# Where ten symmetry tests run: four of them moved from one block's down projection to those of two earlier blocks

## The chip, the cores and the metric

One core of one Trainium2 chip runs the whole program. Its engines work side by side, each through its own list of instructions in order, and wait for each other by semaphores: PE (matrix products into PSUM), DVE and ACT (element-wise work on SBUF and PSUM), POOL (here mostly the issuing of DMAs), SP (DMAs alone). The metric is the device time of one execution in microseconds (us); before the change the median of 3 runs is 1126.09 us (1125.63 to 1129.37).

## The reference

Two equal layers act on x, 2048 tokens of 640 numbers in float32. Each layer is a Fourier mixing and a gated feed-forward network, both behind a layer norm and with a residual:

```
def _A_ref(x, dft_seq_re, dft_seq_im, dft_hid_re, dft_hid_im):
    a = jnp.einsum("bsd,ed->bse", x, dft_hid_re)
    b = jnp.einsum("bsd,ed->bse", x, dft_hid_im)
    return jnp.einsum("ts,bse->bte", dft_seq_re, a) - jnp.einsum("ts,bse->bte", dft_seq_im, b)

def _B_ref(x, w_gate, w_up, w_down):
    g = jnp.einsum("bsd,df->bsf", x, w_gate)
    u = jnp.einsum("bsd,df->bsf", x, w_up)
    h = _sigmoid(g) * u
    return jnp.einsum("bsf,fd->bsd", h, w_down)

x = x + _A_ref(_layernorm(x), ...)      # twice, with the same matrices
x = x + _B_ref(_layernorm(x), ...)
```

The two sequence matrices are 2048 x 2048 and come as inputs; F is 1728. The kernel uses that a Fourier matrix repeats itself with changed signs along rows and columns and multiplies by folded, smaller matrices. It tests on the chip that the given matrices have these symmetries: it loads the parts that should be equal up to sign, subtracts or adds them, and sums the squares of what is left. All tests together set one flag at the end; if it says that the symmetry does not hold, a plain, unfolded version runs behind it (with the inputs given it does not). No matrix product waits for a single test.

## The kernel before, in words

**Staging.** A layer has a Fourier part and then a feed-forward part in four blocks of 512 tokens. I count layers and blocks from 1 in the text; the code counts from 0, so that layer 1's blocks are (0, 0) to (0, 3). A block goes through 14 gate and up steps (the products on line 1531; step 0 to 13 of the block) and then through its "down": 8 steps that multiply by the third weight (L1743), two to a row tile of 128 tokens. In layer 1's block 4 two sequence steps stand in between. A down step takes PE 5.6 us; the downs of layer 1 run at about 176 to 220, 300 to 345, 425 to 470 and 553 to 598 us.

**What follows a down.** L1758 on DVE adds each finished row tile from PSUM to X, in two halves. Then the block is folded for layer 2's Fourier part: statistics (L534 and L535, or L768 and L770 for a half), their root on POOL (L516) with small steps around it (L515 to L529), sums and differences of columns (L787, L788), coefficients (L793 and before it L828, L829), scaled rows on ACT (L840, L842) and DVE (L845, L849), and the join (L929 on DVE, L939 on ACT, L949 on DVE), whose result PE multiplies on L1088. In the next block's gate steps L1572, L1580, L1600 on DVE and L1589 on ACT take products out of PSUM and make the gated product of them; L1572 is the one that empties banks for PE.

**The order.** A function at(u, f) puts the job f on a clock of steps: u is a position in PE's order, and each engine gets its instructions in the order of these positions. Nothing else sets the order, neither a cost nor a due time.

**The tests.** The table TESTS gives 84 tests a place: layer, block, step of the load, step of the test, step of the square. The tests stand in a fixed list (32 of rows, 10 of columns, then 32 and 10 again for the second matrix), and the table's entries are given to them in this order. A row test loads 4 x 128 KB by DMAs that POOL issues (L1916), DVE works on them (L1922, L1923, L1925 twice) and ACT squares and sums (L1888). A column test loads 2 x 256 KB (L1933) and has L1939 to L1942 on DVE. Both need a "room" of SBUF for their data from load to square. Two rooms are fixed; if neither is free when a load is placed, one more is taken from the big tile, out of the space where the other tiles live. A later load into a room waits for the test and the square that used it before. All loads stand in order on POOL, all tests in order on DVE.

The table is used here:

```
for (load, test, key), (l, b, u, v, w) in zip(tests, TESTS):
    if l == layer:
        at(block[b] + u, load, *key)
        at(block[b] + v, test, *key)
        at(block[b] + w, square_rest)
```

Where tiles lie in the big tile is found by a planner from the times at which they are taken and dropped. A load by SP into such a place waits for the last user of the place.

Of the kernel before, what the change touches and what calls it, by code (L numbers as in the profile page):

```python
# [80 lines left out]
NP = 6  # L81
MADE = {(1, 1), (1, 2), (1, 3)}
TESTS = [(0, 1, 3.5, 4.9, 5.7), (0, 1, 4.5, 5.9, 6.7), (0, 1, 5.5, 7.1, 7.9), (0, 1, 7.38, 8.97, 9.78), (0, 1, 9.25, 10.85, 11.65), (0, 1, 11.12, 12.72, 13.53),
# [2403 lines left out]
```

## Time and profile before

| | |
|---|---|
| median of 3 runs | 1126.09 us |
| the profiled execution | 1127.29 us |
| its span | 1125.50 us |
| its mean granted clock of TensorE | 0.997 |
| busy: PE, DVE, ACT, POOL | 98%, 73%, 47%, 31% |
| DMA moved | 226.54 MB, 201 GB/s |
| row test loads (L1916), POOL | 256 issues, 128 KB each |
| column test loads, POOL | 32 issues, 256 KB each |

A row of a timeline has the start, the time from the first start to the last end, the engine, the line, the operation, the tiles out<-in with their shapes, the count, and in brackets for how long the engine had been idle before it and what ended that. A row of windows has for each stretch the busy time of each engine, then the granted clock, the mean busy share of the 16 DMA engines and the GB/s moved. A row of waits has the engine, the tile and line that waited, what it waited for, and the us in total, the number of times and the longest. The span of 1125.5 us is what the profile covers; the profiled time is 1.79 us more.

### The profile page before, as it was taken

The page shows a single profiled execution, that of the slowest core. Times are in us where ns is not written, and L with a number is a line of the kernel's source. Part 1 is how long each engine was busy: PE and PEld are TensorE (multiplying, and loading weights), DVE is VectorE, ACT ScalarE, POOL GpSimd, SP SyncE. Part 2 cuts the span into 40 slices and gives each one's busy share as a digit, 9 for nine tenths or more (in the row PEclk, how much of TensorE's full clock was granted, in tenths as well). Part 3 has the DMA queues.
Part 4 walks back from the last instruction along what each step waited for, and adds up shares of the span by engine and source line. Part 5 has one row for each costly group of instructions (what it writes and reads, how often), then busy time and mean ns, then how long its engine had stood idle before and what let it go on. Part 6 is the DMA issues. An engine that isn't in the chain of part 4 may idle for free. (4 is left out here: it accounts for less than half of the span.)

```text
span 1125.5 us, 23738 instructions
## 1 busy us (share of the span) xinstructions
PE 1104.8 (98%) x9004; PEld 881.6 (78%) x9004; DVE 827.2 (73%) x1841; ACT 532.0 (47%) x1153; POOL 345.7 (31%) x568
## 2 busy tenths in 40 slices
PE   7999999999999999999999999999999999999997
PEld 5767446788878887788877878778887888788875
DVE  7984987868877898686568877864887398827962
ACT  6975584245534654255434734422652255415530
POOL 1001654342555445243480202433530214011001
PEclk9999999999999999999999999999999999999999
DMA  7533886889598969977761674598857873398401
GB/s 237 196 103 105 303 295 208 256 260 297 204 220 245 284 208 223 266 258 240 188 200 34 183 201 160 141 254 293 258 153 157 297 244 80 99 259 232 156 7 45
DMA packets 158050, 226.54 MB, mean 201 GB/s; under 512 B 75055, under 2 KB 100161, under 8 KB 157926
## 3 DMA queue, kind: packets, MB, share of 16 engines
q1 hardware_dynamic: 139222, 176.84, 52.3%
q0 software_dynamic: 18560, 47.93, 14.8%
q8 instruction: 72, 1.18, 0.4%
q14 instruction: 52, 0.43, 0.1%
q10 hardware_dynamic: 144, 0.16, 0.0%
HBM read 180.90 MB, written 29.37 MB: 187 GB/s over the span
## 5 line engine op out<-in xcount | busy, mean ns | idle before, releaser
L1531 PE MATMUL acc<-big 128*128 128x256 f16 x4698 | 516.8, 273 | 0.8 <-DMA big<-kept_w 0.4
L1531 PEld LDWEIGHTS <-big 128*128 128x128 f16 x4698 | 459.6, 98 | 55.6 <-issue 0.8
L1916 POOL DMA_DIRECT2D big<-in_ct x256 | 174.3, 687 | 209.5 <-DVE big L1925 121.4
L1743 PE MATMUL acc<-big 128*128 128x320 f16 x1640 | 223.6, 299 | 0.0
L1535 ACT ACTIVATE big<-acc 128x256 f32<-128x256 f32 x268 | 100.7, 381 | 231.4 <-PE acc L1531 220.8
L1743 PEld LDWEIGHTS <-big 128*128 128x128 f16 x1640 | 160.5, 98 | 62.2
L1888 ACT ACTIVATE big<-big 128x768 f32<-128x768 f32 (+9 forms) x110 | 81.3, 739 | 77.6 <-DVE big L1925 61.8
L1484 PE MATMUL acc<-big 128*128 128x256 f16 (+1 forms) x705 | 114.7, 325 | 0.3 <-ACT big L730 0.3
L1788 PE MATMUL acc<-big 128*128 128x320 f16 x756 | 105.6, 299 | 0.0
L1484 PEld LDWEIGHTS <-big 128*128 128x128 f16 x705 | 68.9, 98 | 44.9 <-issue 0.6
L1788 PEld LDWEIGHTS <-big 128*128 128x128 f16 x756 | 74.0, 98 | 28.6
L323 DVE SCALAR_TENSOR_TENSOR big<-big 128x640 f16<-128x640 f32 (+8 forms) x88 | 72.1, 848 | 15.7 <-ACT big L321 10.0
L1589 ACT ACTIVATE big<-big 128x512 f32<-128x512 f32 x87 | 52.8, 628 | 63.1 <-DVE big L1580 62.8
L321 ACT ACTIVATE big<-big 128x640 f16<-128x640 f32 (+8 forms) x88 | 58.6, 698 | 24.6 <-POOL big L1390 10.9
L1600 DVE SCALAR_TENSOR_TENSOR big<-acc,big 128x256 f32<-128x256 f32 x87 | 36.3, 418 | 43.2 <-PE acc L1531 38.6
L1617 DVE TENSOR_TENSOR big<-big 128x512 f16<-128x512 f32 x51 | 35.2, 689 | 42.0 <-ACT big L1616 41.1
L1580 DVE TENSOR_TENSOR big<-big,acc 128x512 f32<-128x512 f32 x87 | 56.2, 679 | 3.2 <-PE acc L1531 2.9
L1808 DVE SCALAR_TENSOR_TENSOR big<-acc,big 128x320 f32<-128x320 f32 x48 | 23.0, 487 | 44.7 <-PE acc L1799 33.1
L494 POOL DMA_INDIRECT out<-big,rows x8 | 8.8, 1105 | 140.5 <-DMA out<-big 53.5
L1641 DVE TENSOR_TENSOR big<-big 128x512 f16<-128x512 f32 x72 | 41.2, 617 | 9.9 <-ACT big L1640 9.9
L673 ACT ACTIVATE big<-big 128x384 f16<-128x384 f32 (+2 forms) x48 | 28.6, 647 | 41.3 <-DVE big L655 29.2
L1572 DVE TENSOR_TENSOR big<-acc,big 128x256 f32<-128x256 f32 x80 | 30.4, 415 | 23.8 <-PE acc L1531 20.8
(268 smaller groups left out, 1312.4 us busy)
## 6 DMA issues: line engine op xcount, KB each, us to landing
big<-kept_s SPq DMA_DIRECT2D x84, 512.0 KB
big<-kept_w SPq DMA_DIRECT2D x115, 320.0 KB
big<-in_ct POOLq DMA_DIRECT2D x256, 128.0 KB, 5.2
big<-kept_w SPq DMA_DIRECT2D x74, 192.0 KB
kept_w<-big SPq DMA_DIRECT2D x27, 320.0 KB
big<-in_ct POOLq DMA_DIRECT2D x32, 256.0 KB, 5.7
big<-in_wd SPq DMA_DIRECT2D x25, 320.0 KB
kept_s<-big SPq DMA_DIRECT2D x13, 512.0 KB
```

The source lines that it names most:

```text
L321: nc.scalar.activation(dh, src, AF.Copy, scale=s)
L323: nc.vector.scalar_tensor_tensor(dl, src, s, dh, op0=OP.mult, op1=OP.subtract)
L1484: nc.tensor.matmul(ps, w[wp][:, d * P : (d + 1) * P], xt[:, xp, :], start=(d == 0 and wp == HI and xp == HI), stop=(d == ND - 1 and wp == LO))
L1531: nc.tensor.matmul(ps, wt, xt, start=start and n == 0, stop=n == len(todo) - 1, skip_group_check=not start)
L1535: nc.scalar.activation(dst, ps, AF.Copy)
L1580: nc.vector.tensor_tensor(v[1], v[1], both, op=OP.add)
L1589: nc.scalar.activation(v, v, AF.Sigmoid, scale=SG)
L1641: nc.vector.tensor_tensor(l, src, h, op=OP.subtract)
L1743: nc.tensor.matmul(held["pd", e][0][:, :EH], held["ht", j].parts[hp][:, i * P : (i + 1) * P], held["w", 2, j].parts[wp][:, e * EH : (e + 1 ...
L1788: nc.tensor.matmul(accs[p, n][0][:, :EH], left(m, q, hp, p), right(m, w, wp), start=start and k == 0, stop=stop and k == len(out) - 1, ski ...
L1888: nc.scalar.activation(v, v, AF.Square, accum_out=new_sum()[:p])
L1916: nc.gpsimd.dma_start(v[:, g], bass.AP(ct.tensor, (r * S + row) * S, [[P, NS], [d * S, 16], [1, P]]))
```

## The change

Four of the ten tests in the down of layer 1's block 4 go: the entries of (0, 2) in the downs become 11 instead of 9, and so do those of (0, 1). Block 4's down keeps six. In the downs of blocks 2 and 3 the distance from one test to the next is 0.82 of a step instead of 1.0; from load to test it is still 1.4 steps, to square 2.2. In block 4's down the loads were half a step apart, with the test 0.7 and the square 1.2 of a step behind; now they are 0.8 apart, the test comes 1.0 and the square 1.5 behind. By these numbers a third room is no longer needed there: the third load, 1.6 steps behind the first, comes after the first one's square.

```
         (0, 1, 13.0, 14.4, 15.2),
-        (0, 1, 14.0, 15.4, 16.2), (0, 1, 15.0, 16.4, 17.2), ... (0, 1, 21.0, 22.4, 23.2),
+        (0, 1, 13.82, 15.22, 16.02), (0, 1, 14.64, 16.04, 16.84), ... (0, 1, 21.18, 22.58, 23.38),
         ...                         (the same lines for (0, 2))
-        (0, 3, 15.6, 16.3, 16.8), (0, 3, 16.1, 16.8, 17.3), (0, 3, 16.6, 17.3, 17.8), (0, 3, 17.1, 17.8, 18.3), ... (0, 3, 20.1, 20.8, 21.3),
+        (0, 3, 15.6, 16.6, 17.1), (0, 3, 16.4, 17.4, 17.9), (0, 3, 17.2, 18.2, 18.7), (0, 3, 18.0, 19.0, 19.5), (0, 3, 18.8, 19.8, 20.3), (0, 3, 19.6, 20.6, 21.1),
```

Since the list of tests is fixed, all tests from the second down on take an earlier place: the third down gets five column tests, where before one stood in it, and the gate steps of block 4 get row tests where column tests stood. PE's order is the same. Many places in the big tile change.

POOL around block 4's down: the loads of tests (L1916), of the hidden matrices' tests (L1976), and L516 of block 4's fold at the end.

```order
-L1916 DMA big<-in_ct 128x2x128 x12
+L1916 DMA big<-in_ct 128x2x128 x28
 L1976 DMA big<-in_wh 100x4x128 x8
-L1916 DMA big<-in_ct 128x2x128 x12
-L1118 MEMSET big 128x2
-L1916 DMA big<-in_ct 128x2x128 x4
-L1118 MEMSET big 128x2 x2
-L1916 DMA big<-in_ct 128x2x128 x24
+L1916 DMA big<-in_ct 128x2x128 x8
+L1118 MEMSET big 128x2 x3
+L1916 DMA big<-in_ct 128x2x128 x16
 L516 TENSOR_TENSOR quad_77<-quad_77,half 128x2 x2
```

Behind the eight loads of L1976 stand 24 loads of row tests (six tests) instead of 40; the first row has more of them, since the columns went earlier.

DVE in block 4's down, behind L1758 of tile 0 and its statistics:

```order
 L534 BN_STATS quad_77<-big 128x6 x2
 L535 BN_AGGR quad_77<-quad_77 128x2
-L1922 TENSOR_TENSOR big<-big 128x256
-L1923 TENSOR_TENSOR big<-big 128x256
-L1925 TENSOR_TENSOR big<-big 128x128 x2
 L1922 TENSOR_TENSOR big<-big 128x256
 L1923 TENSOR_TENSOR big<-big 128x256
```

One of the four tests between tile 0 and tile 1 is gone. Two more are gone ahead of tile 0, and one of two behind L845.

DVE at the end of block 2's down: L1758 of the last tile, and the fold of the block (L534, L787, L793).

```order
 L1758 SCALAR_TENSOR_TENSOR big<-acc_65,big 128x320
 L1758 SCALAR_TENSOR_TENSOR big<-acc_483,big 128x320
-L1922 TENSOR_TENSOR big<-big 128x256
-L1923 TENSOR_TENSOR big<-big 128x256
-L1925 TENSOR_TENSOR big<-big 128x128 x2
 L534 BN_STATS quad_75<-big 128x6 x2
```

Two tests more stand ahead of the L1758 shown here, and the test that stood behind it has gone to a place behind L788.

18 rows, old and new, of the table TESTS are left out of this document.

## The prediction

> **What bounds the kernel now.** I read the page's busy shares first, then the waits of PE, then PE's timeline around its longest wait, then the timelines of the engines that this wait names.
>
> ```profile
> PE 1104.8 (98%) x9004; PEld 881.6 (78%) x9004; DVE 827.2 (73%) x1841; ACT 532.0 (47%) x1153; POOL 345.7 (31%) x568
> ...
> PE acc L1088 <- ACT big L939: 1.4, 1, 1.4
> PE acc L1088 <- DVE big L949: 0.5, 1, 0.5
> ```
>
> PE is busy in 1104.8 of 1125.5 us, so a change that leaves PE's instructions alone can win only PE's idle time and the time for which its clock is low. The diff moves symmetry tests on POOL, DVE and ACT; PE's order is the same. Of the waits inside the program the longest, 1.4 us, lies right behind layer 1's last down, where tests are taken out:
>
> ```profile
> 595.75 2.47 PE L1743 MATMUL acc<-big 128*128 128x320 f16 x17
> 598.06 1.76 PE L1173 MATMUL acc<-big 128*128 128x322 f16 x17
> 599.65 6.07 PE L1088 MATMUL acc<-big 128*128 128x256 f16 x54
> 607.13 0.39 PE L1088 MATMUL acc<-big 128*128 128x256 f16 x2 [1.42 <-ACT big L939]
> 608.02 3.05 PE L1088 MATMUL acc<-big 128*128 128x256 f16 x16 [0.50 <-DVE big L949]
> ...
> 606.00:609.20 3.20, 1.45 (x10) 0.84 (x11) 2.97 (x9) 1.50 (x4) 0.00 (x0) 1.00 0.02 5
> 609.20:612.70 3.50, 3.50 (x20) 2.53 (x18) 3.30 (x8) 2.56 (x6) 0.00 (x0) 0.51 0.00 0
> ```
>
> PE ends the down (L1743) at 598.2, has other work to 605.72, and stands 1.42 + 0.50 us until 608.02; one more small pause of 0.1 us makes 2.0. In the last two rows (time, PE busy, and near the end the granted clock) the clock is 1.00 while PE pauses and 0.51 in the 3.5 us behind it: 3.5 x 0.49 = 1.7 us more. What PE waits for is the fold of block 4, whose last links are these, on DVE and ACT:
>
> ```profile
> 577.84 0.88 DVE L1758 SCALAR_TENSOR_TENSOR big<-acc,big 128x320 f32<-128x320 f32 x2
> 582.95 0.42 DVE L1923 TENSOR_TENSOR big<-big 128x256 f32<-128x256 f32 x1 [1.66 <-DMA big<-in_ct]
> 584.91 0.43 DVE L1923 TENSOR_TENSOR big<-big 128x256 f32<-128x256 f32 x1 [0.67 <-DMA big<-in_ct]
> 587.48 0.43 DVE L1923 TENSOR_TENSOR big<-big 128x256 f32<-128x256 f32 x1 [0.90 <-DMA big<-in_ct]
> 588.36 0.88 DVE L1758 SCALAR_TENSOR_TENSOR big<-acc,big 128x320 f32<-128x320 f32 x2
> 594.38 0.89 DVE L845 SCALAR_TENSOR_TENSOR big<-big,quad 128x641 f32<-128x641 f32 x1 [1.18 <-ACT big L842]
> 595.18 0.42 DVE L1922 TENSOR_TENSOR big<-big 128x256 f32<-128x256 f32 x1
> 596.38 0.42 DVE L1922 TENSOR_TENSOR big<-big 128x256 f32<-128x256 f32 x1
> 597.58 0.88 DVE L1758 SCALAR_TENSOR_TENSOR big<-acc,big 128x320 f32<-128x320 f32 x2
> 601.11 0.47 DVE L1758 SCALAR_TENSOR_TENSOR big<-acc,big 128x320 f32<-128x320 f32 x1
> ...
> 604.80 0.65 ACT L840 ACTIVATE big<-big,coef,quad 128x321 f32<-128x321 f32 x1 [6.11 <-DVE big L793]
> 606.60 0.47 ACT L939 ACTIVATE big<-big 128x321 f16<-128x321 f32 x1
> ```
>
> L1758 adds a finished row tile of the down to X. The last one starts at 601.11, although PE was done at 598.2: DVE runs late, because the tests between its additions (L1922 to L1925) cost it time, and three of them wait 1.66, 0.67 and 0.90 us for their loads. From 601.11 the chain has almost no wait: 601.11 to 606.60 for L939, 607.07 its end, and PE goes on at 607.13.
>
> **The last down: four tests less.** A test takes DVE 596.38 - 595.18 = 1.20 us. DVE's order shows where the four are missing: two ahead of L1758 at 577.84, one of the four between 577.84 and 588.36, one of the two between L845 and 597.58. So L1758 of tile 0 comes at 577.84 - 2.4 = 575.4. Tile 1 follows 10.52 us later in the row, less 1.2 for the test; of the rest up to 3.2 us (1.66 + 0.67 + 0.90) is waiting, which a longer way from load to test can remove. That is 581.5 to 584.7. What the trace does not show is the new rhythm: square comes 1.5 steps after load, loads 0.8 apart, so the two fixed rooms are reused and no third is taken; a load now waits for the square of the test two before it. The price is set by how long a load takes:
>
> ```profile
> 574.87 16.16 POOL L1916 DMA_DIRECT2D big<-in_ct  x24
> ...
> big<-in_ct POOLq DMA_DIRECT2D x26, 128.0 KB, 2.6
> ...
> big<-in_ct POOLq DMA_DIRECT2D x256, 128.0 KB, 5.2
> ```
>
> In 574 to 592 us POOL issues 24 loads without a break, 0.67 each, and they land after 2.6 us (second row, of that window); over the whole program it is 5.2 (third row, the page's). A room's round is four issues, 2.7, the landing, the test, 1.2, and the square on ACT:
>
> ```profile
> 596.55 0.84 ACT L1888 ACTIVATE big<-big 128x768 f32<-128x768 f32 x1 [1.38 <-issue]
> 597.30 0.19 ACT L1888 ACTIVATION_READ_ACCUMULATOR big<-big 128x1 f32 x1
> ```
>
> With the square's 1.0 and a landing of 2.6 that is 7.5 us, two rooms give a test every 3.75, and three tests put tile 1 at 575.4 + 11.2 = 586.6; with 5.2 it is 10.1, 5.05 each, and 590.6. I take 584.7 to 586.6, since the 2.6 is of this very window, which will hold fewer loads. From L1758 to L845 the row needs 594.38 - 588.36 = 6.0, L845 0.8, the one test 1.2, and from tile 2's addition to the last one 601.11 - 597.58 = 3.5: at 586.6 + 11.5 = 598.1 DVE is ready for the last addition just when PE ends. So it starts at 598.3, 2.8 us before 601.11. L939 ends at 604.3, before PE gets there at 605.72. Both gaps go (2.0), and with them the slow clock (1.7), 3.7 in all for PE. DVE and ACT come only some 3.0 us earlier, and they take over a little later:
>
> ```profile
> 615.20 0.89 DVE L1241 SCALAR_TENSOR_TENSOR big<-acc,big 128x322 f32<-128x322 f32 x2
> ...
> 637.40 0.44 PE L722 MATMUL acc<-ident,big 128*128 128x128 f16 x5 [0.17 <-ACT big L730]
> ```
>
> PE's transposes at 637.40 already wait 0.17 us for a chain that starts with L1241; DVE's own queue reaches L1241 no more than 2.8 to 3.1 us earlier. So **-3.0** against this execution, with bounds 0 (tile 1 at 590.6: the last addition at 602.1) and -3.7.
>
> [...]
>
> **The second and third downs: two more tests each.** In the second down DVE's order has 15 tests ahead of the last L1758 instead of 13, and one moves behind the statistics. These loads come when the DMA is full:
>
> ```profile
> 300.30:345.00 44.70, 44.70 (x332) 32.23 (x330) 29.82 (x70) 14.60 (x28) 23.73 (x35) 1.00 0.95 247
> 424.80:469.50 44.70, 44.70 (x332) 32.23 (x330) 30.68 (x71) 14.82 (x28) 21.24 (x31) 1.00 1.06 232
> ...
> 337.33 0.43 DVE L1923 TENSOR_TENSOR big<-big 128x256 f32<-128x256 f32 x1 [1.62 <-DMA big<-in_ct]
> 342.26 0.43 DVE L1923 TENSOR_TENSOR big<-big 128x256 f32<-128x256 f32 x1 [1.52 <-DMA big<-in_ct]
> 342.72 0.49 DVE L1925 TENSOR_TENSOR big<-big 128x128 f32<-128x128 f32 x2
> 344.90 0.89 DVE L1758 SCALAR_TENSOR_TENSOR big<-acc,big 128x320 f32<-128x320 f32 x2 [1.69 <-PE acc L1743]
> 345.71 0.42 DVE L1922 TENSOR_TENSOR big<-big 128x256 f32<-128x256 f32 x1
> 353.07 0.71 DVE L1572 TENSOR_TENSOR big<-acc,big 128x256 f32<-128x256 f32 x2
> ...
> 344.84 27.35 PE L1531 MATMUL acc<-big 128*128 128x256 f16 x249
> ...
> 469.38 0.89 DVE L1758 SCALAR_TENSOR_TENSOR big<-acc,big 128x320 f32<-128x320 f32 x2 [1.79 <-PE acc L1743]
> ```
>
> DVE itself has room: 2 x 1.2 us beside 44.7 - 29.8 = 14.9 idle. The bytes have none: the DMA share of the second down is 0.95 at 247 GB/s. Two tests are 2 x 4 x 128 KB = 1.05 MB, 4.2 us. I take all of it as delay of the last L1758, since every load is in order on POOL: 349.1 instead of 344.9. Behind that addition DVE still has the statistics and then L1572, which empties two banks of the next block's first gate step; it moves from 353.78 (its end) to 358.0. PE needs these banks after 120 matmuls of L1531, at 344.84 + 120 x 27.35 / 249 = 358.0. So the slack, 4.2 us, is used up just about: **+0.3**, between 0 (bytes fit into gaps) and 4.0 (below). In the third down five tests of columns come where row tests were; DVE waits 1.79 us for PE at 469.38 and the work moved behind is the same L534 to L1572, so 4.2 + 1.8 stand against a like delay: I take 0, with the second down's upper bound.
>
> The tests' addresses move too, so kept blocks loaded by SP wait for other tests than before; such loads stand 4 us or more ahead of their use in what I looked at, and I cost them at nothing; if that cover is gone, the load's lateness falls on PE one to one.
>
> **The sum.** This execution took 1127.29 us, span 1125.50 and 1.79 around it: 1127.29 - 3.0 + 0.3 = 1124.6. The median, 1126.09, lies 1.2 below the profiled one and the fastest 1.66, about what the slow clock costs, so I take the unprofiled runs for ones without it; for them only the 2.0 us of gaps are there to win: 1126.09 - 2.0 + 0.3 = 1124.4. I say **1124.5**.
>
> **Rivals.** *All of it:* the gaps and the clock are won against the median too: 1126.09 - 3.7 = 1122.4. For it: the slow clock stands in the one trace there is. Against it: the fastest run's 1125.63.
>
> *No gain:* two rooms make the tests bound by latency, 5.2 us per load instead of 2.6; tile 1 comes at 590.6, the last L1758 at 602.1, and the wait at L939 stays: 1126 to 1127. For it: three waits for in_ct in the rows of that stage. Against it: that window's 2.6.
>
> *The slow clock has another cause* than the pause, and stays when the gaps go: 1127.29 - 2.0 + 0.3 = 1125.6 in a profiled run. For it: PE was busy for 1.45 of the 3.2 us ahead of the slow stretch, so it was never long idle. Against it: the stretch starts right behind the pauses, and the stage before it has 1.00. [...]
>
> *Slower:* DVE, which is in order, waits in the second down for test loads while the last L1758 stands behind them. The two tests at 337.33 and 342.26 are 4.93 us apart. If the two added ones keep that pace, the last ends at 343.2 + 9.9 = 353.1, L1758 is 8.2 late, and L1572 passes PE's 358.0 by 4.0; a pause longer than the one at 607 brings the slow clock again, 1.7. That is 1124.3 + 5.7 = 1130.0. It decides from a delay of 4.2 us at L1758. For it: the share of 0.95. Against it: the test at 345.71 found its data without a wait.
>
> **How the numbers follow.** Forecast 0.52, all of it 0.10, no gain 0.18, clock stays 0.08, slower 0.12. What a measurement of this kernel can tell from no change is 0.3%, 3.4 us: below 1122.7 is faster, above 1129.5 slower. The forecast, no gain and the clock's case lie within: same 0.78. Faster 0.11 is "all of it" with a little over; slower 0.11 the most of the last. The likeliest case alone reaches from 1123.2 to 1126.0; the range, with no gain and most of the stall's sizes, from 1122.0 to 1128.2.
>
> **What would show it.** Right: no wait of PE at L1088 for L939 or L949, the clock at 1.00 in 606 to 613, the last L1758 of the last down within 0.5 us of PE's end, L1758 of the second down around 349 with a PE pause at L1531 under 1 us. Wrong: PE's wait at L1088 as before (then the two rooms), a pause of PE over 2 us at the start of block 3 (then the full DMA), or a wait for kept blocks somewhere else.

## The result, and the profile after

The changed kernel takes 1143.12 us (median of 4 runs, 1139.85 to 1144.47) against 1126.91 us for the kernel before (4 runs, 1125.63 to 1129.37): a ratio of 1.0137, with an interval of 1.0108 to 1.0165. It is 16 us slower, and the forecast was 1124.5, with a range up to 1128.2. The profiled span is 1141.4 us, 15.9 more than before.

The waits of PE after the change (the line that waits, what it waits for, us in total, times, longest) show where the time is:

```profile
PE acc L1531 <- ACT big L1535: 12.4, 6, 5.2
PE acc L1088 <- DMA big<-kept_o: 1.5, 1, 1.5
PE acc L1531 <- DVE big L1572: 1.2, 2, 1.0
```

Before, L1531 waited 0.4 us for L1572 and never for L1535, and there was no wait for kept_o. L1531 are the gate and up products; ACT's L1535 empties their PSUM. The two waits at L1088 for L939 and L949, which the change was to remove, are gone. The next views are windows of the second down, of block 3's gate and up steps, of the third down and of block 4's steps, first of the kernel after:

```profile
300.00:344.70 44.70, 44.70 (x332) 32.23 (x330) 29.10 (x68) 15.53 (x30) 24.45 (x36) 1.00 0.92 227
344.70:433.60 88.90, 82.09 (x733) 72.32 (x732) 70.58 (x170) 45.46 (x100) 42.12 (x74) 0.98 0.80 241
433.60:478.30 44.70, 44.70 (x332) 32.23 (x330) 25.37 (x58) 13.55 (x25) 17.38 (x25) 1.00 0.82 168
478.30:566.90 88.60, 82.58 (x734) 72.66 (x733) 65.96 (x161) 45.92 (x105) 36.52 (x57) 0.96 0.83 258
```

and of the kernel before, the two stretches of gate and up steps (its two downs stand in the prediction):

```profile
345.00:424.80 79.80, 79.80 (x733) 71.49 (x732) 67.43 (x161) 45.40 (x98) 36.33 (x67) 1.00 0.78 241
469.50:549.40 79.90, 79.90 (x734) 71.62 (x733) 58.78 (x140) 43.95 (x97) 27.15 (x43) 1.00 0.74 241
```

The downs themselves take PE 44.70 us as before, without a pause. Block 3's steps take 88.90 instead of 79.80 (+9.1), block 4's 88.60 instead of 79.90 (+8.7), by pauses and by a lower granted clock (0.98 and 0.96 for 1.00). One thing is odd: the downs that were given more tests moved *less*. In the second it is 227 x 44.7 = 10.1 MB for 11.0 before (247), in the third 7.5 MB for 10.4 (168 and 232 GB/s). The loads came late; the mean DMA share was no higher than before (0.92 for 0.95, and 0.82 for 1.06).

PE's timeline of the kernel after, at the starts of blocks 3 and 4 and behind the last down:

```profile
348.92 9.98 PE L1531 MATMUL acc<-big 128*128 128x256 f16 x90 [0.95 <-ACT big L1535]
359.92 4.75 PE L1531 MATMUL acc<-big 128*128 128x256 f16 x42 [1.01 <-DVE big L1572]
365.23 11.95 PE L1531 MATMUL acc<-big 128*128 128x256 f16 x108 [0.57 <-ACT big L1535]
381.46 22.79 PE L1531 MATMUL acc<-big 128*128 128x256 f16 x192 [4.29 <-ACT big L1535]
...
486.77 16.90 PE L1531 MATMUL acc<-big 128*128 128x256 f16 x132 [5.20 <-ACT big L1535]
504.50 5.73 PE L1531 MATMUL acc<-big 128*128 128x256 f16 x51 [0.82 <-ACT big L1535]
...
617.24 1.76 PE L1173 MATMUL acc<-big 128*128 128x322 f16 x17
618.83 8.04 PE L1088 MATMUL acc<-big 128*128 128x256 f16 x72
...
652.49 0.44 PE L722 MATMUL acc<-ident,big 128*128 128x128 f16 x5 [0.18 <-ACT big L730]
```

Behind the last down all is as hoped: the 72 products of L1088 run through from 618.83, and from L1173 to the marked L722 it is 652.49 - 617.24 = 35.25 us, where before it was 637.40 - 598.06 = 39.34. That is 4.1 gained. Together with the wait for kept_o this gives 9.1 + 8.7 + 1.5 - 4.1 = 15.2 of the 15.9 us. In block 3 the pauses add up to 0.95 + 1.01 + 0.57 + 4.29 = 6.82, in block 4 to 5.20 + 0.82 = 6.02. Of the other 2.3 and 2.7 of their 9.1 and 8.7, 1.7 and 2.3 are PE at a granted clock of 0.50 (from 382.14 to 385.55, and behind the pause of 5.20 up to 491.37); 0.6 and 0.4 are left unexplained.

**How the second down reaches PE.** DVE of the kernel after:

```profile
350.58 0.43 DVE L1923 TENSOR_TENSOR big<-big 128x256 f32<-128x256 f32 x1 [0.95 <-DMA big<-in_ct]
...
351.45 0.88 DVE L1758 SCALAR_TENSOR_TENSOR big<-acc,big 128x320 f32<-128x320 f32 x2
...
359.48 0.71 DVE L1572 TENSOR_TENSOR big<-acc,big 128x256 f32<-128x256 f32 x2
...
376.65 0.43 DVE L1922 TENSOR_TENSOR big<-big 128x256 f32<-128x256 f32 x1 [5.21 <-DMA big<-in_ct]
378.33 0.42 DVE L1923 TENSOR_TENSOR big<-big 128x256 f32<-128x256 f32 x1 [1.25 <-DMA big<-in_ct]
...
454.57 1.13 DVE L655 TENSOR_SCALAR big<-big,small 128x640 f32<-128x640 f32 x2 [8.38 <-DMA big<-big]
...
490.57 0.88 DVE L1758 SCALAR_TENSOR_TENSOR big<-acc,big 128x320 f32<-128x320 f32 x2
...
617.44 0.49 DVE L1758 SCALAR_TENSOR_TENSOR big<-acc,big 128x320 f32<-128x320 f32 x1 [3.57 <-PE acc L1743]
```

The last addition of the second down starts at 351.45 (344.90 before), behind a test that waits for its load. PE starts block 3 at nearly the same time in both kernels (344.53 and 344.84), so DVE has come 6.5 us late to it. The lateness then goes through three engines that each work in order. ACT of the kernel after:

```profile
347.66 0.84 ACT L1888 ACTIVATE big<-big 128x768 f32<-128x768 f32 x1 [3.06 <-DVE big L1925]
...
348.50 0.64 ACT L1535 ACTIVATE big<-acc 128x256 f32<-128x256 f32 x2
...
379.91 1.23 ACT L1589 ACTIVATE big<-big 128x512 f32<-128x512 f32 x2 [7.77 <-DVE big L1580]
...
485.52 0.84 ACT L1888 ACTIVATE big<-big 128x768 f32<-128x768 f32 x1 [0.75 <-DVE big L1942]
```

First, the square of a late test (L1888) stands ahead of L1535, which empties the banks of the new block's first products: ACT waits 3.06 us for DVE's test, so L1535 comes at 348.50 and PE at 348.92. In block 4 it is the same: the last of several late squares starts at 485.52, and PE has paused 5.20 us when L1535 has come. Second, L1572 comes at 359.48, and PE, after 30 + 90 products, waits 1.01 for it. Third comes POOL. Its timeline of the kernel after:

```profile
319.60 2.03 POOL L1916 DMA_DIRECT2D big<-in_ct  x3 [3.43 <-ACT big L1888]
326.07 5.40 POOL L1916 DMA_DIRECT2D big<-in_ct  x8 [4.44 <-issue]
...
359.67 0.20 POOL L515 TENSOR_SCALAR quad<-quad 128x4 f32<-128x4 f32 x1 [7.94 <-DVE quad L535]
...
368.07 5.50 POOL L1916 DMA_DIRECT2D big<-in_ct  x8
```

and of the kernel before:

```profile
320.23 4.72 POOL L1916 DMA_DIRECT2D big<-in_ct  x7 [2.06 <-ACT big L1888]
...
353.25 0.19 POOL L515 TENSOR_SCALAR quad<-quad 128x4 f32<-128x4 f32 x1 [9.64 <-DVE quad L535]
...
360.77 5.49 POOL L1916 DMA_DIRECT2D big<-in_ct  x8
```

POOL does the root of the fold (from L515, with the steps to L829), and behind it, in order, the loads of block 3's next tests. The root waits for DVE's statistics (L535), so the eight loads go out at 368.07 instead of 360.77; the test they are for waits on DVE until 376.65 and again until 378.33; L1580 stands behind it, then ACT's L1589 and L1535, and PE pauses 4.29 us at 381.46. So one late load in the down became a late load 40 us further on, through DVE's and POOL's order.

**What makes the first load late.** In the rows of POOL above, seven loads go out in a row from 320.23 before: the last three of one test and the four of the next, which start at about 322.2. In the kernel after the three go out at 319.60, then POOL stands for 4.44 us, and the next test's loads start at 326.07. They go into an additional room. The planner has put it where the tile of a pair (L655 to L674: two row tiles of a later block, normalised, split into two parts and then transposed by DMA) had lain until one tick of the planner's clock before. The pair's last instruction, L674, is at 324.58, itself behind such transposes (5.31 us of waiting ahead of it). The profile names no releaser for the 4.44 us; that it is this place is shown by e9 below, where L674 comes later still, at 326.06, and the loads don't wait for it. In the third down it is turned about: L655 at 454.57, the start of the second pair, waits 8.38 us for a DMA, since its tile's new place overlaps one that the first pair's transposes still read, and tests and additions stand behind it. The last L1758 there starts at 490.57, when PE left the down at 478.3.

### The profile page after: what moved, and what is told of

Its sections match the earlier page's. It is cut to its first block, busy times and chain, and to the rows that moved or that the text cites. A ratio compares the mean times of both kernels' runs of the same rounds, so it can differ in the third digit from the quotient of the medians.

```text
span 1141.4 us, 23714 instructions
## 1 busy us (share of the span) xinstructions
PE 1108.4 (97%) x9004; PEld 883.2 (77%) x9004; DVE 826.8 (72%) x1841; ACT 529.4 (46%) x1153; POOL 349.3 (31%) x568
## 5 line engine op out<-in xcount | busy, mean ns | idle before, releaser
L1531 PE MATMUL acc<-big 128*128 128x256 f16 x4698 | 521.6, 274 | 13.6 <-ACT big L1535 12.4
L1531 PEld LDWEIGHTS <-big 128*128 128x128 f16 x4698 | 461.5, 98 | 71.2 <-issue 15.0
L1916 POOL DMA_DIRECT2D big<-in_ct x256 | 174.7, 688 | 248.9 <-DVE big L1925 133.6
L1535 ACT ACTIVATE big<-acc 128x256 f32<-128x256 f32 x268 | 98.9, 380 | 202.1 <-PE acc L1531 176.7
L1888 ACT ACTIVATE big<-big 128x768 f32<-128x768 f32 (+9 forms) x110 | 81.3, 740 | 96.4 <-DVE big L1925 69.5
L1589 ACT ACTIVATE big<-big 128x512 f32<-128x512 f32 x87 | 52.8, 628 | 76.6 <-DVE big L1580 75.0
L1580 DVE TENSOR_TENSOR big<-big,acc 128x512 f32<-128x512 f32 x87 | 56.2, 679 | 3.2 <-PE acc L1531 2.9
L1572 DVE TENSOR_TENSOR big<-acc,big 128x256 f32<-128x256 f32 x80 | 30.4, 415 | 24.3 <-PE acc L1531 24.3
```

The costliest lines, as they stand in the source:

```text
L1531: nc.tensor.matmul(ps, wt, xt, start=start and n == 0, stop=n == len(todo) - 1, skip_group_check=not start)
L1535: nc.scalar.activation(dst, ps, AF.Copy)
L1580: nc.vector.tensor_tensor(v[1], v[1], both, op=OP.add)
L1589: nc.scalar.activation(v, v, AF.Sigmoid, scale=SG)
L1888: nc.scalar.activation(v, v, AF.Square, accum_out=new_sum()[:p])
L1916: nc.gpsimd.dma_start(v[:, g], bass.AP(ct.tensor, (r * S + row) * S, [[P, NS], [d * S, 16], [1, P]]))
```

## The experiments

Three theories were held against each other: that DVE and DMA have too little room for two more tests in a down (**bytes and work**); that one engine's order carries a lateness to PE which one wait starts (**order**); and that the places of tiles, which the change redistributes, make loads wait (**places**). The table gives all runs. "Lag" is the time from 0.11 us ahead of PE's last product of a down to the start of the last two L1758 (0.31 where DVE waits for PE); "loss" how much longer than 79.8 us the gate and up steps of the next block are on PE. Lags and losses are from one profiled execution each, the times and ratios from all runs beside runs of the kernel before, whose median was between 1125.8 and 1126.9 beside the several groups, so that a difference between runs of two groups is good to about 1 us.

| run | median us | ratio [95%] | lag 2nd down | loss block 3 | lag 3rd down | loss block 4 |
|---|---|---|---|---|---|---|
| before | 1126.9 | | 0.31 | 0 | 0.31 | 0 |
| after | 1143.1 | 1.0137 [1.0108, 1.0165] | 7.16 | 9.1 | 12.67 | 8.7 |
| e1 | 1122.3 | 0.9968 [0.9957, 0.9979] | 0.31 | 0 | 0.31 | 0 |
| e3 | 1122.7 | 0.9965 [0.9950, 0.9979] | 0.31 | 0 | 0.31 | 0 |
| e4 | 1135.1 | 1.0067 [1.0046, 1.0087] | 8.12 | 11.7 | 0.92 | 0 |
| e5 | 1129.0 | 1.0017 [1.0008, 1.0027] | 0.31 | 0 | 8.70 | 4.7 |
| e2 | 1139.0 | 1.0113 [1.0086, 1.0139] | 7.30 | 10.1 | 4.44 | 0.45 |
| e6 | 1132.2 | 1.0056 [1.0037, 1.0076] | 4.78 | 6.5 | 3.36 | 0 |
| e7 | 1141.9 | 1.0130 [1.0110, 1.0150] | 8.11 | 10.7 | 12.66 | 8.7 |
| e8 | 1125.4 | 0.9996 [0.9978, 1.0013] | 12.33 | 10.1 | 1.87 | 0 |
| e9 | 1131.5 | 1.0052 [1.0033, 1.0070] | 5.81 | 6.7 | 0.31 | 0 |
| e10 | 1126.3 | 0.9996 [0.9987, 1.0006] | 4.63 | 0.64 | 0.31 | 0 |
| e11 | 1133.0 | 1.0058 [1.0041, 1.0074] | 0.31 | 0 | 0.31 | 0 |
| n1 | 1122.9 | 0.9972 [0.9960, 0.9983] | 0.31 | 0 | 3.85 | 0 |
| n2 | 1128.8 | 1.0027 [1.0004, 1.0049] | 0.31 | 3.0 | 2.48 | 0.74 |

In most of them each entry of the table of tests has the number of its test in front, so that a test can be left out or moved without moving the others:

```
-for (load, test, key), (l, b, u, v, w) in zip(tests, TESTS):
+for (load, test, key), l, b, u, v, w in ((tests[n], *t) for n, *t in TESTS):
```

### The last down alone (e1)

The second and third downs as before, the last down's six tests at the new places, four tests left out.

```
 (0, 1) and (0, 2): the nine places of before, (13.0, 14.4, 15.2), (14.0, 15.4, 16.2), ... (21.0, 22.4, 23.2)
-(0, 3, 15.6, 16.3, 16.8), (0, 3, 16.1, 16.8, 17.3), ... (0, 3, 20.1, 20.8, 21.3)          ten
+(0, 3, 15.6, 16.6, 17.1), (0, 3, 16.4, 17.4, 17.9), ... (0, 3, 19.6, 20.6, 21.1)          six
```

> Only the last down is changed: six tests there, 0.8 of a step apart, test 1.0 and square 1.5 behind the load; the other four of its ten tests are left out altogether. Second and third downs, and the order in which the tests take their places, are as before. Theory A (the two tests added to each of the second and third downs cost all that was lost): the last down's part is a gain by itself, 2 to 4 us under the kernel before, 1123 to 1125, no wait of PE at L1088 for L939, none above 0.6 us in blocks 3 and 4. Rival (the new rhythm with two rooms costs itself): 1127 or more, L1758 of the last down late as before.

1122.3 us, a ratio of 0.9968: 3.6 us faster (2.4 to 4.8). PE, DVE and the window behind the pause, in its profile:

```profile
599.38 8.04 PE L1088 MATMUL acc<-big 128*128 128x256 f16 x72
```

```profile
597.99 0.49 DVE L1758 SCALAR_TENSOR_TENSOR big<-acc,big 128x320 f32<-128x320 f32 x1 [0.70 <-PE acc L1743]
```

```profile
607.20:610.60 3.40, 3.40 (x38) 2.80 (x36) 3.37 (x7) 3.40 (x9) 0.00 (x0) 1.00 0.00 0
```

The last addition waits for PE; the pauses are gone and the clock stays at 1.00 where it was 0.51. So this part of the change brings what was hoped of it, and the whole loss is made by where the four tests went. Whether it is the smaller number of tests or the new places that bring it, e1 does not tell; e11 bears on that.

### Nine and nine, but with the moved kinds of tests (e3)

As the change, with the downs' nine places of before and four tests left out, so that column tests stand in the third down as in the change.

```
 as after; in (0, 1) and (0, 2) the nine places of before, the tests 15, 16, 35 and 36 left out
```

> The changed kernel with second and third downs back at nine tests a whole step apart; the four tests that were added there are left out. The rest of the list keeps the places of the changed kernel, so five tests of columns sit in and behind the third down instead of where they were before. Theory A: as e1, 1123 to 1125. Rival (the moved kinds of test, columns instead of rows and the reverse, cost something by themselves): above 1127, with waits of PE in block 4 and none in block 3.

1122.7 us, like e1. That column tests stand where row tests stood costs nothing that the two runs could tell (the prediction took it as 0).

### One down at a time (e4, e5)

```
 e4: (0, 1) eleven places of the change;  (0, 2) nine places of before, tests 35 and 36 left out
 e5: (0, 1) nine places of before, tests 15 and 16 left out;  (0, 2) eleven places of the change
```

> The changed kernel with eleven tests in the second down, and the third down back at nine a whole step apart (its two added ones left out). Places in the big tile are such that in the third down L655 of the second pair still has to wait for the transposes of the first pair, as in the changed kernel. Theory A (number of tests per down): block 3 loses about 9 us as in the changed kernel, block 4 nothing: 1123.5 + 9 = 1132 to 1134. Theory B (in block 4 it is the place: L655 waits 8.4 us for the transposes and holds the tests behind it): block 4 loses as well, 5 to 8 us, in all 1138 to 1141.

> The changed kernel with eleven tests in the third down, and the second down back at nine a whole step apart (its two added ones left out). Here L655 of the second pair in the third down doesn't wait for transposes. Theory A: block 3 loses nothing, block 4 about 8.6 us: 1131 to 1134. Theory B: block 4 loses at most 2 us, 1123 to 1126.

e4 takes 1135.1 and e5 1129.0. Against e3's 1122.7 the second down costs 12.4 and the third 6.3; together 18.7 of the change's 20.5. e5 lies between the two times that were expected. Beside block 3's loss e4 has waits of its own in layer 2 (2.6 us for a kept block, 0.7 and 1.1), and its profile is of the longest of its four runs (1140.9; the others 1131.7 to 1135.3), so it isn't a clean piece. It decides one question. DVE of e4 in the third down:

```profile
457.74 1.13 DVE L655 TENSOR_SCALAR big<-big,small 128x640 f32<-128x640 f32 x2 [7.91 <-DMA big<-big]
```

The long wait of L655 is there, and with nine tests behind it block 4 loses nothing. In e5, with eleven, L655 does not wait (1.13 us at 439.57), and block 4 loses 4.7. So the theory that this wait alone makes the third down's loss fell. With the wait and the added tests together, in the change, the lag is 12.67.

### The two downs without the relief in the last one (e2)

The two downs as in the change, the last down's ten at their old places (four tests run twice, 88 in all).

```
 (0, 1) and (0, 2): the eleven places of the change
+(0, 3, 15.6, 16.3, 16.8), (0, 3, 16.1, 16.8, 17.3), ... (0, 3, 20.1, 20.8, 21.3)          ten, as before
```

> The changed kernel with eleven tests in each of the second and third downs, but the last down with ten tests at the old places (six of them its own, four repeated, so four tests more in all). L655 of the second pair in the third down doesn't wait for transposes here. Theory A: the last down's gain of 4.5 is lost, the downs' loss stays: 1143 + 4.5 = 1147. Theory B (part of the loss in block 4 is the wait for transposes, as 6.3 us of the third down alone against 8.6 in the changed kernel let expect): 1143 to 1145, with waits of PE at the start of block 4 of 4 us instead of 6.

1139.0 us, 1.0113, under both times that were expected. Block 3 loses 10.1 again, block 4 only 0.45: with this table the third down's last addition lags 4.44, not 12.67. A new wait of 3.3 us for a load of the hidden matrices stands at 566, ahead of the last down. The parts do not add up (by the medians +13.2 here and -4.6 in e1 make +8.6, and the change has +16.2): a difference of 8.2 us in block 4 between two kernels with the same two downs pointed to the places of tiles, which differ.

### The loads or the work (e6, e7)

Both take four row tests of the two downs, the eighth and ninth of the second down's eleven and the fifth and sixth of the third's. e6 keeps their rooms, DVE's work and the squares and leaves out their loads (the squares go to a spare sum). e7 keeps their loads and leaves out their work on DVE and ACT.

```
+if key in ((0, 13), (0, 14), (0, 30), (0, 31)):
+    load, test = new_room, test_stale        # e6
+    test = no_test                           # e7
```

> The changed kernel, but four row tests (the eighth and ninth of the second down's eleven, the fifth and sixth of the third's) load nothing: room, DVE's work and ACT's square stay, on what lies in the room, and the square goes into a sum of its own. It leaves out 16 loads of 128 KB. Theory L (what costs is that DVE waits in order for late loads): the last addition in the second down comes 4 us earlier or more, PE's waits at the start of block 3 fall from 6.8 us to under 2: 1126 to 1133. Theory W (DVE's and ACT's own work and order): as the changed kernel, 1141 to 1144.

> The changed kernel, but the same four tests only load: DVE's work on them and ACT's square are left out, and the room is free at once. The bytes are as in the changed kernel. Theory L: nobody waits for these loads any more, so as with no loads, or a little slower since the bytes still delay the loads behind them: 1126 to 1135. Theory Q (the bytes on a full DMA hold the kept blocks and all other loads, whoever waits): 1139 to 1144, with waits for other loads.

e7 takes 1141.9, hardly less than the change; e6 1132.2. So the work of four tests on DVE and ACT costs next to nothing by itself, and without their loads 10.9 of the 20.5 go. But 9.5 are left over e3. PE's timeline of e6 has the pause at the test behind the root still:

```profile
380.40 23.85 PE L1531 MATMUL acc<-big 128*128 128x256 f16 x205 [4.36 <-ACT big L1535]
```

By these two runs alone the bytes could still be half of the loss. e9 and e10, which load every byte of the change, decide against that: e10 is 3.7 us above e3.

### Only the places (e9, e11)

Rooms from the third on are asked for twelve ticks of the planner's clock earlier, so that a room is not put where something lay until just before its load. Every engine's instructions and their order stay those of the change (e9) or of the kernel before (e11).

```
-self.asked.append([n, self.clock, None, ...])
+self.asked.append([n, self.clock - 12 * (high == LATE), None, ...])
```

> The changed kernel with every engine's instructions and their order unchanged; only the places of tiles in the big tile differ: the planner has to keep the place of an additional room (third and later ones) free for 12 of its ticks before the room is taken. In the changed kernel the second down's third room lies where the second pair's tile lay until one tick before, and the third down's likewise, so that their loads wait for the pair's last user behind the transposes. Theory P (places): the loads at 326.07 and 460.50 come some us earlier, the last additions are at most 4.5 us behind PE's end, PE's waits in blocks 3 and 4 fall from 12.8 us to under 4: 1122 to 1130. Theory L (eleven tests are more bytes than a down's DMA takes beside the kept blocks): 1138 to 1144 as the changed kernel.

> The kernel before with all instructions and orders unchanged and only the places of tiles found anew, by the rule that the place of an additional room is free for 12 ticks before. If places cost only where a room is taken right behind a held tile: as the kernel before, 1125 to 1128, no wait of PE above 0.6 us in blocks 3 and 4. If any new set of places costs some us by itself: above 1129.

e9 takes 1131.5: 11.7 us less than the change by places alone (9.6 by the two ratios). POOL and the waits of PE in its profile:

```profile
320.38 4.71 POOL L1916 DMA_DIRECT2D big<-in_ct  x7 [3.57 <-ACT big L1888]
```

```profile
PE acc L1531 <- ACT big L1535: 5.4, 3, 3.2
```

Seven loads go out in a row from 320.38 again, as before the change (320.23), without the stop of 4.44 us behind the third. Block 4's loss is gone; in block 3 a pause of 1.54 at the start and one of 3.20 behind the root stay. So to cost the addresses at nothing was wrong by about half of the loss.

e11 was to show that the same shift does no harm where no room lies badly. It did harm: 1133.0, 6 us slower than the kernel with the same instructions in the same order. Blocks 3 and 4 of layer 1 lose nothing (0.08 and 0); a new pause stands in layer 2. DVE and PE of e11:

```profile
756.43 0.42 DVE L1922 TENSOR_TENSOR big<-big 128x256 f32<-128x256 f32 x1 [5.98 <-DMA big<-in_ct]
```

```profile
764.01 4.21 PE L1531 MATMUL acc<-big 128*128 128x256 f16 x19 [5.86 <-ACT big L1535]
```

A late load again, a test in DVE's order, and PE 5.86 us behind it, in another block. So places cost a kernel with no added test some us too, and my narrower reading of e9 (that they cost only with more tests in a down) fell. Which set of places is good can't be told from the number of tests.

The same shift of places also did some good, and that bears on the last down. POOL, DVE and PE of e11 there:

```profile
572.71 16.14 POOL L1916 DMA_DIRECT2D big<-in_ct  x24
```

```profile
598.94 0.47 DVE L1758 SCALAR_TENSOR_TENSOR big<-acc,big 128x320 f32<-128x320 f32 x1
```

```profile
599.93 8.21 PE L1088 MATMUL acc<-big 128*128 128x256 f16 x72
```

All ten tests stand in this down as in the kernel before. But their 24 loads start 2.2 us earlier than there (574.87), so does the last L1758 (601.11 there), and PE's 72 products of L1088 run through: the two pauses that the change was to remove are gone with no test removed. So places made part of that pause too. How much of e1's gain is the smaller number of tests, and how much its own new places, is not shown.

### Two loads ahead of the root (e10)

e9, and the loads of block 3's second and third tests moved ahead of the fold's root on POOL.

```
-(0, 2, 1.5, 2.9, 3.7), (0, 2, 2.5, 3.9, 4.7),
+(0, 2, 1.4, 2.9, 3.7), (0, 2, 1.45, 3.9, 4.7),
```

> The changed kernel with the places as in the run with rooms free earlier, and on POOL the loads of two tests of block 3's first gate steps ahead of the root of block 2's fold (L515, L516) instead of behind it and behind its coefficients (to L829). Nothing else moves. Theory R (the wait of 3 to 5 us at about 380 is a test whose load stands on POOL behind the fold, which waits for the late last addition): that wait falls under 1 us, block 3's loss from 6.7 to 2 to 4 us, in all 1126 to 1129. If it is the DMA being full there: as before it, 1130 to 1133.

1126.3 us, 5.1 less than e9 and level with the kernel before (0.9996). DVE and the waits of PE:

```profile
348.91 0.90 DVE L1758 SCALAR_TENSOR_TENSOR big<-acc,big 128x320 f32<-128x320 f32 x2
...
368.50 0.42 DVE L1922 TENSOR_TENSOR big<-big 128x256 f32<-128x256 f32 x1
```

```profile
PE acc L1531 <- ACT big L1535: 0.5, 1, 0.5
```

The test that waited 5.21 us at 376.65 finds its data at 368.50 without a wait, and of the 12.4 us of PE's wait for L1535 0.5 are left. The last L1758 is at 348.91, 4.0 later than before, and that costs 0.64 us. The planner gives e10 the same places as e9, tile for tile, and the traces have the same instructions in the same order on every other engine, so the difference is POOL's order (5.1 us by the medians, 6.3 by the ratios). The pause at the block's start is shorter as well (0.45 for 1.54); the loads that it hangs on stand ahead of the moved ones, so that part of the two profiles' difference is not the edit's doing.

### Squares or tests moved behind the block's start (e8, n2)

e8 moves the squares of the downs' last three tests behind the next block's first steps; n2 moves their tests too.

```
 e8: -(0, 1, 19.55, 20.95, 21.75), (0, 1, 20.36, 21.76, 22.56), (0, 1, 21.18, 22.58, 23.38), (0, 2, 0.5, 1.9, 2.7)
     +(0, 1, 19.55, 20.95, 23.7), (0, 1, 20.36, 21.76, 24.2), (0, 1, 21.18, 22.58, 24.5), (0, 2, 0.5, 1.9, 2.9)
 n2: +(0, 1, 19.55, 22.1, 22.9), (0, 1, 20.36, 22.9, 23.7), (0, 1, 21.18, 23.7, 24.5), (0, 2, 0.95, 2.3, 3.1)
     (the same for (0, 2) and (0, 3))
```

> The changed kernel with ACT's squares of each down's last three tests behind the next block's first L1535, where the changed kernel has two of them ahead. Theory S (PE's waits for L1535 at 348.9 and 486.8, 0.95 and 5.2 us, are squares ahead of L1535 in ACT's order): these two waits go, but L1572 is as late as before on DVE and takes most of it over: total 1138 to 1143, with waits for L1572 of 3 us or more in both blocks. If the squares alone are to blame: under 1136.

> The changed kernel with the last three tests of each of the two downs (DVE and square) behind the down's last addition, one after it, one behind the statistics, one in the next block's second step; loads stay where they are, the next block's first one 0.45 of a step later. All tests done. Theory D (the last addition waits in DVE's order behind tests whose loads are late): the last addition is at most 3 us behind PE's end, 13 tests ahead as in the kernel before: 1122 to 1127. Theory P or L: the late loads are only met further behind, by L1572 or L1580: 1130 to 1142.

e8 was expected at 1138 to 1143 and takes 1125.4; two of its ten times lie at 1132.9, the others at 1123.2 to 1127.0, and its profile is of a long one (span 1131.1, block 3's loss 10.1), so the trace does not show the median's behaviour. n2 takes 1128.8, between the two times that were expected, with five times at 1125.7 to 1127.5 and five at 1130.1 to 1134.2. Both hold rooms longer, so their places differ from the change's, and e9 showed that places alone move 11.7 us. What the squares ahead of L1535 cost by themselves is left open; that ACT waits 3.06 us in a square ahead of L1535 is a reading of the trace.

### The four tests in layer 2's last block (n1)

The downs' nine places, the last down's six, and the four row tests where the last block of layer 2 has room.

```
+(1, 3, 12.0, 14.3, 14.8), (1, 3, 13.0, 14.9, 15.4), (1, 3, 14.4, 15.6, 16.1), (1, 3, 14.9, 16.3, 16.8)
```

> All tests done: the kernel before with the last down's six as in the change, and the other four row tests in layer 2's last block, loads at its steps 12 to 15, tests and squares from 14.3 to 16.8 behind its gate steps, ahead of the sum over all tests at step 18. There the DMA share is 0.08 to 0.32 and POOL has no other loads. If the price of the change is the place of the four tests: as with them left out, 1121.5 to 1123.5. If four tests cost wherever they are: 1126 or more.

1122.9 us, 0.9972 (0.9960 to 0.9983), with all 84 tests: faster than the kernel before and 20 us faster than the change. They run on DVE from 1082.80 to 1090.1, and one of them waits, in this row of DVE's timeline:

```profile
1089.22 0.42 DVE L1923 TENSOR_TENSOR big<-big 128x256 f32<-128x256 f32 x1 [0.45 <-DMA big<-in_ct]
```

The wait is 0.45 us. Over e1, which leaves the four out, the tests cost 0.6 us, less than the two ratios can tell apart.

## Why the prediction was wrong

The time was 16 us over the one before, and the forecast 2 us under it. By the runs, from e3 (nine and nine, 1122.7) to the change (1143.1) there are 20.5 us. Places are 11.7 of them (after to e9), the loads behind the root on POOL 5.1 (e9 to e10), and 3.7 are what is left to e3, of it 1.2 a wait for a kept block in e10. By the ratios, each beside runs of the kernel before, the three are 9.6, 6.3 and 3.5. The order of these steps matters, since the causes need each other: without the loads of four tests 10.9 go as well (e6).

Step by step:

- **The last down.** Right in what goes: the last L1758 waits for PE (3.57 us at 617.44), and both gaps and the slow clock behind them are gone, in e1 and in the change. I took -3.0 against the profiled execution and measured -4.1: DVE's takeover at 637.40, which I let eat 0.7, moved along. That it takes four tests less is not shown: in e11 the same gaps go with all ten tests, by places alone.
- **"I take the unprofiled runs for ones without it"**, the slow clock. Wrong, at least in part. The gaps alone were 2.0; e1 is 3.6 us faster over all runs (2.4 to 4.8). By the granted clocks on record (each to 0.001 of a run, 1.1 us) 60 runs of the kernel before lose 2.7 us on average and 21 of e1, e3 and n1 1.9; by this estimate 0.8 of the slow clock's 1.7 us are in the mean run, and with the gaps 2.8 of the 3.6 are found. For the last down the rival "all of it", at 1122.4, had the right number, e1 is 1122.3, but its sum is not shown.
- **"The slow clock has another cause".** That rival fell: without the pause the window 607.20 to 610.60 has 1.00.
- **The rule for the slack in the second down** held as far as it was tested. I said that L1758 can be 4.2 us late before L1572 passes PE's need after 120 products. A lag of 0.31 is no delay, so a lag of 4.63 (e10) is 4.3 late: PE loses 0.64 there, and 0.45 and 0 with lags of 4.44 and 3.85 in the third down (e2, n1). PE did wait for L1572 after 30 + 90 products, at 359.92.
- **The size of the delay there**, taken as 4.2 us of bytes, was 6.5. It isn't bytes: the down moved less than before (227 GB/s for 247), and 247 was no ceiling, since block 4's steps after the change moved 258 and the page of the kernel before has a slice of the span with 303. Its loads were held on POOL until a place came free. With the pace of the tests I had a rival for in-order waits, at 8.2 late and 5.7 us; its engine and its threshold were right, and its price was made at one wait, L1572. That wait is 1.0. The price lies in what I did not follow: the squares on ACT ahead of L1535, and above all POOL, where the root waits for DVE and the next loads wait for the root (4.29 at 381.46).
- **The third down, taken as 0.** Wrong by 8.7 us in the change. I let the 1.8 us that DVE waits for PE add to the slack and looked at nothing ahead of it, where L655's place now makes it wait 8.38.
- **"The tests' addresses move too ... I cost them at nothing."** This is the step that failed most. I looked at SP's loads of kept blocks, which do cost 1.5 us at L1088, and not at the loads on POOL, nor at DVE's own writes into places that a DMA still reads. 11.7 us of the loss go with places alone.

What the clock adds is read behind the pauses: a granted clock of 0.50 from 382.14 to 385.55 behind the 4.29, and up to 491.37 behind the 5.20, which is 1.7 and 2.3 us of PE. In the kernel before the clock was 0.50 from 609.24 on, behind 3.41 us in which PE had been busy for 1.49.

## What to carry to other kernels

A table that moves work moves addresses as well. Before costing that at nothing, find for every load and every written tile who last used its new place, and when that user ends; a load that waits there holds the loads behind it on its engine (here POOL stood for 4.44 us). And where an in-order engine both computes and issues loads, a lateness of its computation is paid again where those loads are used (here 4.29 us of PE at 381.46), so follow a delay through every engine's order, not only to the first wait of PE. A run that moves addresses alone tells how much of a difference is theirs, in the kernel before as well.

## What the runs showed of the hardware

**Pauses and TensorE's clock.** In these runs the length of a pause did not decide whether the clock fell. In e2 PE pauses 3.29 us (the wait for the hidden matrices, up to 566.09) and its clock stays at 1.00; in e4 it pauses 2.61 us (for a kept block, up to 826.81), and the clock behind it is 0.50. In the traces of the kernels before and after the granted clock is 1.00 or 0.50. The slow stretches of the kernel after start at 382.14, 484.54 and 1136.48; the second and the third start 30 and 191 times 3.413 us behind the one ahead of them. The two that end before the program does are 3.41 and 6.83 us long, and the one behind the pauses of the kernel before is 3.41 us long, from 609.24. So the windows here have this length and lie along those times. Of the kernel after (a pause of 4.29 us):

```profile
378.72:382.14 3.42, 0.68 (x7) 0.60 (x7) 3.38 (x10) 2.23 (x5) 1.48 (x3) 1.00 1.05 257
382.14:385.55 3.41, 3.41 (x19) 2.41 (x17) 3.38 (x8) 2.80 (x7) 2.46 (x4) 0.50 1.06 293
```

of e2 (3.29) and of e4 (2.61):

```profile
561.24:564.66 3.42, 1.56 (x15) 1.14 (x12) 2.34 (x5) 2.42 (x5) 1.29 (x2) 1.00 1.04 186
564.66:568.07 3.41, 1.99 (x18) 1.78 (x19) 2.65 (x5) 1.01 (x2) 2.12 (x2) 1.00 0.86 150
568.07:571.48 3.41, 3.41 (x28) 2.45 (x26) 1.35 (x5) 2.37 (x9) 3.41 (x6) 1.00 0.97 238
...
823.14:826.55 3.41, 1.06 (x10) 0.70 (x8) 3.34 (x11) 0.38 (x1) 1.13 (x2) 1.00 1.10 299
826.55:829.97 3.42, 3.16 (x15) 2.24 (x16) 3.35 (x10) 1.66 (x4) 0.00 (x0) 0.50 1.01 284
```

In e2 the pause lies across two of these windows, PE is busy for 1.56 and 1.99 us of them (the number behind the length in a row; the clock is the third from the end), and the clock stays at 1.00. In e4 it lies in one but for its last 0.26 us, with 1.06 us of work, and the next one is at 0.50. In the kernel before PE is busy for 1.49 us from 605.82 to 609.24, around its two pauses, and the next 3.41 us are at 0.50. In the traces of the kernels before and after, the windows at 1.00 that are followed by 0.50 have 0.11 to 1.49 us of work (two of the five are the last ones with work in their program), and those followed by 1.00 have 1.87 or more. No limit for other kernels is shown by so few. From 382.14 to 385.55, at 0.50, PE has 19 products in its row, and in the 3.41 us behind it, at 1.00, it has 33; I estimate that such a stretch costs PE up to half of its length, 1.7 us.

**Places alone.** The same instructions in the same order on every engine took 1143.1 and 1131.5 us with two sets of places, and in the kernel before 1126.9 and 1133.0, though there the new places also took away the pause behind the last down. I had not thought that a set of addresses can weigh 1% of a tuned kernel.
